# A filter-then-SiLU kernel: the first batch's rows stored in two halves, the second batch's x loaded ahead of the weights, weight rounding moved between steps

## The chip, the cores and the metric

The kernel runs on one core of a Trainium2 chip. The metric is the device time of one execution in microseconds (us); the median of three runs of the kernel before is 2508.29 us (2508.0 to 2508.46). One more execution was taken under the hardware profiler; the lines and times below are of that one, counted from the start of its span.

## What is computed

Two blocks follow one another. The first filters x along its 3008 positions in the frequency domain, the second is a feed-forward block with SiLU on every row of the result:

```python
X = np.fft.rfft(x, axis=1)                       # x: (8, 3008, 256)
y = np.fft.irfft(X * (filt_r + 1j * filt_i), n=3008, axis=1)
h = y.reshape(8 * 3008, 256) @ w_in              # w_in: (256, 2048)
out = (h / (1 + np.exp(-h))) @ w_out             # w_out: (2048, 256)
```

x and the filter are single precision, the weights arrive as double precision and are rounded to single precision on the chip.

## The kernel before, in words

**Main loop.** After a start of some 60 us, TensorE runs 384 steps (`hidden` and `project`, L966 and L1025): 8 batches, two halves each, three blocks of token pairs per half, eight steps of weights per block. A step multiplies by `w_in` with seven products in place of eight (sums of blocks are formed on VectorE), applies SiLU on ScalarE, and multiplies by `w_out`, one step behind. VectorE adds the sums that TensorE's next product waits for (L950). Every engine executes its own instructions in program order, so whatever is written between two of them is in the way of the later one.

**Filter of the next batch.** It is cut into pieces that are written into the steps by hand: `put(step, round, piece)` places a piece at one of eight rounds of a step. The filter is a transform in two stages with a filter product between: stage 1 (matmuls into tiles `pa`), rows stored to DRAM (`d1`) and loaded turned, `forward` (`pb`), `multiply`, `inverse` (`pc`), rows stored to DRAM (`d2`) and loaded turned (tiles `t4`), and `stage3` (`pd`), whose result y feeds the main loop.

**First batch.** Nothing runs beside it, so its chain is on the way to step 0. Its six groups g go through `inverse_first` and `rows_first` (L664): two tiles of 128 partitions per group are copied out of PSUM and stored to `d2`, 256 KB each. The first 32 positions split into two halves, n below 16 and n from 16. `load_t4_rows(k)` (L699, L703) loads the first half only, three loads of two DMAs, from SP (k = 0 and 2) and POOL (k = 1). `stage3(0..3)` then makes the first half of y. The second half of `d2` is loaded by `load_t4(g)` from step 8 on (L694).

**Order of DMA issues around it.** SP issues the tables, weights 0 to 3, then the second batch's x for two stage-1 pieces (`load_two`, L405), then weights 4 and 5 (L1302 to L1315). Stores of `rows_first` go out on ScalarE's queue, and for two tiles on SP's. While `d2` is stored and loaded TensorE runs a filler, `idle(11, small=20)` (L1362): products whose result nobody reads.

**After pd.** POOL copies one element of y to `gate` (L1365), so that its later DMAs stay behind y. Then it issues `store_rows(0)` and `store_rows(1)` (L426, L429): the stage-1 rows of the second batch, four DMAs of 96 KB each per piece. The tiles t1 that they read come from a pool of two. Piece u = 2 of stage 1 (TensorE L416, ScalarE copies L421) stands in step 1, one more piece in each step up to step 6. Its copy into t1 needs the first t1 tile back, that is, the landing of the four DMAs of `store_rows(0)`. SP meanwhile issues x for u = 2, weights 6 and 7, x for u = 3, weights 8, 9 and 10.

**Rounding of weights.** Weights 4 to 15 are rounded during steps 0 to 9, in pieces on VectorE: `bits` (two instructions), `added`, `signed`, `placed` (one each; `rounded` is `added` and `signed`), with `converted` on ScalarE, and `combine_weights` (four additions) for each pair. The table that places them is at L1382 to L1397.

**Semaphores of DMAs.** There are eight of them for the hardware queues (SP and ScalarE together) and eight for POOL's, used in turn. A DMA waits until the one that had its semaphore before has landed.

Of the kernel before, what the change touches and what calls it, by code (L numbers as in the profile page):

```python
# [46 lines left out]
FP32 = mybir.dt.float32  # L47
# [6 lines left out]
B, S, C = 8, 3008, 256  # L54
DFF = 2048
N1, N2 = 47, 64
NS, NG = 24, 6
# [106 lines left out]
def dft_tables():  # L164
# [22 lines left out]
    n = np.arange(32)[:, None]  # L187
    for par in range(2):
        for i, idx in enumerate(ORDER):
# [3 lines left out]
            k = np.where((kap - sp) % 94 == 0, kap, S - kap)  # L193
# [5 lines left out]
    e = np.zeros((4, 32, NG, 2, 2, 2, 32))  # L199
    n = np.arange(32)[None, :]  # L200
    for g in range(NG):
        for bank in range(2):
            for j in range(4):
# [3 lines left out]
                k = np.where((kap - s) % N1 == 0, kap, S - kap)[:, None]  # L207
# [57 lines left out]
def kernel(  # L265
# [9 lines left out]
    nc = tc.nc  # L275
# [84 lines left out]
    def spectral(b):  # L360

        if b > 0:
            d1 = dpool.tile([2, NS, 2, 32, C], FP32, name=f"d1_{b}", tag="d1")
        d2 = dpool.tile([2 * NS, 32, 2, C], FP32, name=f"d2_{b}", tag="d2")
        xs, us, t2s, banks, prods, halves, t4s = {}, {}, {}, {}, {}, {}, {}
# [298 lines left out]
        def rows_first(g):  # L664

            if g in (2, 3):
                room = t4pool.tile([128, 4, C], FP32, name=f"q_{b}_{g}", tag="t4")
                tiles = room[:, 0:2], room[:, 2:4]
            else:
                tiles = [pool.tile([128, 2, C], FP32, name=f"q_{b}_{g}_{i}", tag=tag) for i, (pool, tag) in  # L670
                         enumerate(((zpool, "z"),) * 2 if g == NG - 1 else ((qpool, "q"), (opool, "o")))]
            for i, qt in enumerate(tiles):
                copy, queue = (nc.scalar.copy, nc.scalar) if i == 0 or g < 4 else (nc.scalar.copy if g == 4 else nc.vector.tensor_copy, nc.sync)
                copy(out=qt, in_=halves[g][i])
                a0 = 8 * g + 4 * i
                queue.dma_start(out=d2[a0:a0 + 4].rearrange("a n h c -> (a n) h c"), in_=qt)

# [16 lines left out]
        def load_t4(g):  # L694
            t4s[g] = t4pool.tile([128, 4, C], FP32, name=f"t4_{b}_{g}", tag="t4")
            for h in range(2):
                nc.sync.dma_start(out=t4s[g][64 * h:64 * h + 2 * NS], in_=d2[:, 4 * g:4 * g + 4, h, :])

        def load_t4_rows(k, queue=None):  # L699

            first, by = SPREAD[k]
            for h in range(2):
                (queue or nc.sync).dma_start(out=us["t4"][64 * h + first:64 * h + first + 15 * by + 1:by],  # L703
                                  in_=d2[16 * k:16 * k + 16, 0:16, h, :])

# [34 lines left out]
        def load_wide(k):  # L740
            t4s[k] = [t4pool.tile([128, 8, C // 2], FP32, name=f"t4_{b}_{k}_{cb}", tag="t4") for cb in range(2)]
            for cb in range(2):
                for r in range(4):
                    nc.sync.dma_start(
                        out=t4s[k][cb][32 * r:32 * r + 24],
                        in_=d2[r % 2::2, 8 * k:8 * k + 8, r // 2, 128 * cb:128 * cb + 128])

# [31 lines left out]
        def fold_wide(k, h):  # L779
# [3 lines left out]
            for at, n, op in ((0, 24, ALU.add), (24, 23, ALU.subtract)):  # L783
                nc.vector.tensor_tensor(out=dst[:, :, :, at:at + n], in0=even[:, :, :, 0:n], in1=odd[:, :, :, 0:n], op=op)

        return dict(us=us, store_rows=store_rows, evict_y=evict_y, halves=halves, load_first=load_first, stage1_first=stage1_first, load_x=load_x, load_two=load_two, stage1=stage1, reverse_x=reverse_x,
                    load_fold=load_fold, fold=fold, stage1_fold=stage1_fold, evict_fold=evict_fold, pairs_fold=pairs_fold, forward_two=forward_two, free_two=free_two, multiply_two=multiply_two, add_two=add_two, inverse_two=inverse_two, even_two=even_two, rows_two=rows_two, ends_two=ends_two,
# [436 lines left out]
    def weights(*js, queue=None):  # L1224
        for j in js:
            if wide:
                load_weights(j, queue)
# [73 lines left out]
    nc.sync.dma_start(out=wi_t, in_=ws_dram.ap())  # L1301
    weights(0, 1, 2, 3)  # L1302

# [8 lines left out]
    for j in range(4):  # L1312
        part["stage1_first"](j)
    second["load_two"]()
    weights(4, 5)  # L1315
    part["forward"](0, fill=12)
# [44 lines left out]
    placed(2, 3)  # L1361
    idle(11, small=20)  # L1362
    for g in range(4):
        part["stage3"](g)
    gp.tensor_copy(out=gate, in_=y[0, 0][:, 0, 28:29])  # L1365
    for u in range(2):
        second["store_rows"](u)
    idle_wide(1)
    nc.sync.dma_start(out=wi_t, in_=wi_dram.ap())
    second["load_x"](2)  # L1370
    weights(6, 7)
    second["load_x"](3)
    early[0] = None
    plan_rest(0, part)
# [7 lines left out]
    for step, rnd, *todo in (  # L1382
            (0, 1, (combine_weights, 1), (bits, 4)), (0, 5, (converted, 4), (bits, 5), (added, 4)),
            (1, 0, (converted, 5), (weights, 8, 9, 10)), (1, 1, (signed, 4), (placed, 4), (rounded, 5), (placed, 5)),
            (1, 5, (combine_weights, 2)),
            (2, 1, (bits, 6), (added, 6)), (2, 5, (converted, 6), (bits, 7)), (3, 0, (converted, 7)),
            (3, 1, (signed, 6), (placed, 6), (added, 7)), (3, 5, (signed, 7), (placed, 7)), (3, 7, (bits, 8)),
            (4, 0, (converted, 8), (weights, 11)), (4, 1, (rounded, 8), (placed, 8), (bits, 9)), (4, 2, (weights, 12)),
            (4, 5, (converted, 9), (added, 9), (bits, 10)), (5, 0, (converted, 10), (weights, 13)),
            (5, 1, (signed, 9), (placed, 9), (rounded, 10), (placed, 10)),  # L1390
            (5, 5, (combine_weights, 3)), (5, 7, (bits, 11)), (6, 0, (converted, 11), (weights, 14, 15)),
            (6, 1, (rounded, 11), (placed, 11), (bits, 12)), (6, 5, (converted, 12), (combine_weights, 4)),
            (6, 7, (bits, 13)), (7, 0, (converted, 13)),
            (7, 1, (rounded, 12), (placed, 12), (rounded, 13)), (7, 5, (combine_weights, 5)), (7, 7, (bits, 14)),
            (8, 0, (converted, 14)), (8, 1, (placed, 13), (rounded, 14), (placed, 14), (bits, 15)),
            (8, 5, (converted, 15), (combine_weights, 6)),
            (9, 1, (rounded, 15), (placed, 15)), (9, 5, (combine_weights, 7))):  # L1397
        for piece, *args in todo:
            put(step, rnd, piece, *args)
# [7 lines left out]
    for pair in range(len(pairs)):  # L1407
        step, rnd = combines[pair % per] if pair not in (1, 2) else ((2, 1), (11, 5))[pair - 1]
        pending.append((pair // per * STEPS + step + rnd / ROUNDS, 98, lambda pair=pair: tokens(pair)))
        for chunk in range(2 if pair < len(pairs) - 1 else 0):  # L1410
            step, rnd = stores[pair % per][chunk] if pair > 1 else (stores[1 - pair][chunk] if pair == 0 else (13, 1 + 4 * chunk))
            pending.append((pair // per * STEPS + step + rnd / ROUNDS, 99 + chunk,
                            lambda pair=pair, chunk=chunk: output(pair, chunk)))
# [65 lines left out]
```

## Time and profile before

| | us |
|---|---|
| median of three runs | 2508.29 |
| the profiled execution | 2507.81 |
| its span | 2506.0 |
| TensorE busy in the span | 2485.5 |
| VectorE busy | 1758.7 |
| ScalarE busy | 1097.1 |
| POOL busy | 433.3 |
| last pd product of the start ends | 59.41 |
| first product of step 0 starts | 60.15 |

The profile gives for each engine its busy time and, for each instruction, when it ran, on which line, from which tiles to which, and what ended the idle time before it. A single-precision product appears as two matmul records, so "x22" is 11 products. Queue q1 holds SP's DMAs, q10 ScalarE's and q0 POOL's. "SPq", "ACTq" are the sequencers that issue DMAs. The trace also holds each DMA packet with its queue, start and size, and each landing of a DMA as an update of its semaphore.

### The profile page before, as it was taken

The page shows a single profiled execution, that of the slowest core. Times are in us where ns is not written, and L with a number is a line of the kernel's source. Part 1 is how long each engine was busy: PE and PEld are TensorE (multiplying, and loading weights), DVE is VectorE, ACT ScalarE, POOL GpSimd, SP SyncE. Part 2 cuts the span into 40 slices and gives each one's busy share as a digit, 9 for nine tenths or more (in the row PEclk, how much of TensorE's full clock was granted, in tenths as well). Part 3 has the DMA queues.
Part 4 walks back from the last instruction along what each step waited for, and adds up shares of the span by engine and source line. Part 5 has one row for each costly group of instructions (what it writes and reads, how often), then busy time and mean ns, then how long its engine had stood idle before and what let it go on. Part 6 is the DMA issues. An engine that isn't in the chain of part 4 may idle for free.

```text
span 2506.0 us, 42288 instructions
## 1 busy us (share of the span) xinstructions
PE 2485.5 (99%) x16240; PEld 2126.6 (85%) x16240; DVE 1758.7 (70%) x3608; ACT 1097.1 (44%) x3006; POOL 433.3 (17%) x675
## 2 busy tenths in 40 slices
PE   8999999999999999999999999999999999999999
PEld 6678888888888888888888888888888888888988
DVE  6876677777767777777777867777677767655544
ACT  3644444444444444444444444444444444444443
POOL 3211212112121121211222112211121111101100
PEclk9999999999999999999999999999999999999999
DMA  7523232213232032420324203321142211200000
GB/s 277 181 69 98 71 83 63 77 51 80 60 88 77 26 90 51 116 65 16 88 66 106 57 26 85 84 68 43 31 108 56 55 43 34 64 21 9 17 9 17
DMA packets 139705, 170.67 MB, mean 68 GB/s; under 512 B 20892, under 2 KB 112892, under 8 KB 138876
## 3 DMA queue, kind: packets, MB, share of 16 engines
q1 hardware_dynamic: 115536, 120.49, 18.3%
q0 software_dynamic: 22240, 44.63, 6.9%
q8 instruction: 127, 2.08, 0.4%
q10 hardware_dynamic: 1728, 2.87, 0.3%
q14 instruction: 74, 0.61, 0.1%
HBM read 96.06 MB, written 81.26 MB: 71 GB/s over the span
## 4 chain that ended last, share of the span: by engine, by line
PE 97%; DVE 2%; ACT 0%; DMA 0%; issue 0%; POOL 0%; SPq 0%; DVEq 0%; ACTq 0%
PE acc L1047 45%; PE px L979 26%; PE pyz L979 19%; PE pd L754 1%; PE pf L486 1%; PE pc L582 1%; PE pb L544 1%; DVE g L950 0%; PE pa L392 0%; PE pc L660 0%; PE pa L416 0%; PE pd L718 0%; PE pb L526 0%; DMA w_t<-d 0%; PE pc L640 0%
## 5 line engine op out<-in xcount | busy, mean ns | idle before, releaser
L1047 PE MATMUL acc<-g,w_t 128*128 128x256 f32 (+1 forms) x5376 | 1507.7, 376 | 3.0 <-ACT o L767 2.5
L1047 PEld LDWEIGHTS acc<-g,w_t 128*128 128x128 f32 x5376 | 1016.0, 190 | 154.4 <-ACT o L767 15.3
L950 DVE TENSOR_TENSOR g<-pyz,abc 128x256 f32<-128x256 f32 (+1 forms) x1152 | 479.2, 416 | 475.1 <-ACT abc L1000 237.0
L950 DVE TENSOR_TENSOR g<-g 128x256 f32<-128x256 f32 (+3 forms) x1152 | 589.8, 512 | 196.8 <-ACT g L983 183.7
L979 PE MATMUL px<-ty,w_t 128*128 128x256 f32 (+1 forms) x2304 | 676.0, 375 | 0.6 <-ACT abc L1000 0.5
L983 ACT ACTIVATE g<-g 128x256 f32<-128x256 f32 (+1 forms) x1152 | 472.9, 411 | 239.3 <-DVE g L950 239.3
L950 POOL TENSOR_TENSOR s<-s 128x256 f32<-128x256 f32 (+1 forms) x322 | 247.1, 785 | 1386.1 <-DVE s L1073 991.4
L979 PEld LDWEIGHTS px<-ty,w_t 128*128 128x128 f32 x2304 | 434.0, 190 | 58.1 <-issue 3.7
L979 PE MATMUL pyz<-y,w_t 128*128 128x256 f32 (+1 forms) x1536 | 451.7, 376 | 3.7 <-DVE g L950 3.6
L979 PEld LDWEIGHTS pyz<-y,w_t 128*128 128x128 f32 x1536 | 283.0, 189 | 48.6 <-DVE g L950 8.5
L994 ACT COPY abc<-px 128x256 f32<-128x256 f32 (+1 forms) x384 | 141.5, 369 | 367.7 <-PE px L979 367.7
L983 ACT ACTIVATE g<-px 128x256 f32<-128x256 f32 (+1 forms) x384 | 146.0, 380 | 298.7 <-PE px L979 298.6
L1000 ACT COPY abc<-px 128x256 f32<-128x256 f32 (+1 forms) x384 | 141.7, 369 | 307.8 <-PE px L979 307.7
L979 PE MATMUL px<-y,w_t 128*128 128x256 f32 (+1 forms) x768 | 227.4, 378 | 0.9 <-ACT g L983 0.8
L979 PE MATMUL pyz<-ty,w_t 128*128 128x256 f32 (+1 forms) x768 | 226.0, 376 | 0.6 <-DVE g L950 0.6
L979 PEld LDWEIGHTS px<-y,w_t 128*128 128x128 f32 x768 | 143.4, 189 | 24.5 <-ACT g L983 3.3
L979 PEld LDWEIGHTS pyz<-ty,w_t 128*128 128x128 f32 x768 | 141.9, 190 | 23.0 <-DVE g L950 3.0
L987 ACT COPY abc<-px 128x256 f32<-128x256 f32 (+1 forms) x384 | 135.5, 353 | 36.2 <-PE px L979 36.2
L506 POOL DMA_DIRECT2D d<-tf x96 | 48.6, 506 | 212.7 <-DVE tf L436 212.7
L1073 ACT COPY s<-acc 128x512 f32<-128x512 f32 (+1 forms) x92 | 53.1, 577 | 46.5 <-issue 28.1
L603 POOL DMA_DIRECT2D d<-low x36 | 22.3, 618 | 291.8 <-DVE low L599 286.1
L476 DVE TENSOR_TENSOR uf<-x_all 120x512 f32<-120x512 f32 (+1 forms) x72 | 60.2, 863 | 0.3 <-issue 0.3
(130 smaller groups left out, 1359.7 us busy)
## 6 DMA issues: line engine op xcount, KB each, us to landing
t<-d SPq DMA_DIRECT2D x84, 256.0 KB
t<-d SPq DMA_DIRECT2D x224, 96.0 KB
out_dram<-s SPq DMA_DIRECT2D x62, 256.0 KB
d<-q POOLq DMA_DIRECT2D x48, 256.0 KB, 5.2
x_all<-in_x_dram SPq DMA_DIRECT2D x96, 96.0 KB
x_all<-xr SPq DMA_DIRECT2D x96, 96.0 KB
d<-tf POOLq DMA_DIRECT2D x96, 96.0 KB, 2.7
d<-tq POOLq DMA_DIRECT2D x96, 96.0 KB, 2.9
```

The costliest lines, as they stand in the source:

```text
L476: nc.vector.tensor_tensor(out=out, in0=in0, in1=in1, op=op)
L486: nc.tensor.matmul(out=ps[q][32 * k:32 * k + 32], lhsT=wq_t[rows, k], rhs=rhs[k][rows], start=True, stop=True)
L506: nc.gpsimd.dma_start(out=d1[par, :, grp, at:at + 4], in_=part[rows].rearrange("p q n c -> p (q n) c"))
L544: nc.tensor.matmul(out=ps[k, ri][32 * j:32 * j + 32, a, :], lhsT=dn_t[rows, 4 * (g + a) + at, :], rhs=t2s[g + a][rows, at, :], start=True, ...
L950: eng.tensor_tensor(out=out, in0=in0, in1=in1, op=op)
L979: nc.tensor.matmul(out=out, lhsT=w_t[:, jp, c, 0], rhs=rhs, start=start, stop=True, skip_group_check=True)
L983: nc.scalar.activation(out=g[:, k, 0:n], in_=g[:, k, 0:n] if src is None else src, func=AFT.Silu)
L987: nc.scalar.copy(out=sums[:, 0, 0:n], in_=xo)
L994: nc.scalar.copy(out=sums[:, 1, 0:n], in_=xo)
L1000: nc.scalar.copy(out=sums[:, 2, 0:n], in_=xo)
L1047: nc.tensor.matmul(out=acc[pair][i][:, h, 0:n], lhsT=w_t[:, jp, OUT_PLACE.get(c, c), 1], rhs=g[:, k, 0:n], start=(new and h == 0), stop=la ...
L1073: copy(out=dst, in_=src)
```

## The change

`rows_first` keeps its tiles and stores only the even partitions (the first half of the positions, since the table e is permuted so that the two halves alternate). A new `store_half(g, i, 1, gp)` stores the odd partitions from POOL, for all twelve tiles, after `gate` and ahead of `store_rows`. `d2` of the first batch has the half as its leading index. For the second batch, which shares the table e, `load_wide` picks every other row. The tiles of groups 4 and 5 sit in other pools or in free space of `w_t`.

`load_two` moves ahead of weights 0 to 3, weights 4 and 5 follow those directly. Of SP's loads after pd, x for u = 3 now comes ahead of weights 7. Weights 7 and 8 use tiles of the pool t4 that the tiles of groups 2 and 3 occupy until both halves are stored. The filler becomes 24 small and 6 larger products in place of 20 and 11. The table of rounding pieces is rewritten.

```diff
-    n = np.arange(32)[None, :]
+    n = np.arange(32).reshape(2, 16).T.reshape(1, 32)
...
-        d2 = dpool.tile([2 * NS, 32, 2, C], ...)
+        d2 = dpool.tile([2 * NS, 32, 2, C] if b else [2, 2 * NS, 16, 2, C], ...)
...
         def rows_first(g):
...
+            us["q", g] = tiles
             for i, qt in enumerate(tiles):
...
                 copy(out=qt, in_=halves[g][i])
-                a0 = 8 * g + 4 * i
-                queue.dma_start(out=d2[a0:a0 + 4].rearrange("a n h c -> (a n) h c"), in_=qt)
+                store_half(g, i, 0, queue)
+
+        def store_half(g, i, half, queue):
+
+            a0 = 8 * g + 4 * i
+            queue.dma_start(out=d2[half, a0:a0 + 4].rearrange("a n h c -> (a n) h c"), in_=us["q", g][i][half::2])
...
+            first = 16 * (k % 2) + k // 2
+            rows = slice(8 * k, 8 * k + 8) if b > 1 else slice(first, first + 15, 2)
...
     nc.sync.dma_start(out=wi_t, in_=ws_dram.ap())
-    weights(0, 1, 2, 3)
+    second["load_two"]()
+    weights(0, 1, 2, 3, 4, 5)
...
-    second["load_two"]()
-    weights(4, 5)
     part["forward"](0, fill=12)
...
-    idle(11, small=20)
+    idle(6, small=24)
     for g in range(4):
         part["stage3"](g)
     gp.tensor_copy(out=gate, in_=y[0, 0][:, 0, 28:29])
+    for g in (2, 3, 4, 5, 0, 1):
+        for i in range(2):
+            part["store_half"](g, i, 1, gp)
     for u in range(2):
         second["store_rows"](u)
...
     second["load_x"](2)
-    weights(6, 7)
+    weights(6)
     second["load_x"](3)
+    weights(7)
...
-            (1, 5, (combine_weights, 2)),
-            (2, 1, (bits, 6), (added, 6)), (2, 5, (converted, 6), (bits, 7)), (3, 0, (converted, 7)),
...
+            (1, 3, (bits, 6), (added, 6)), (1, 5, (converted, 6), (combine_weights, 2)),
+            (2, 1, (signed, 6), (placed, 6), (bits, 7), (added, 7)), (2, 5, (converted, 7), (bits, 8), (weights, 11)),
...
-            (7, 1, (rounded, 12), (placed, 12), (rounded, 13)), (7, 5, (combine_weights, 5)), (7, 7, (bits, 14)),
-            (8, 0, (converted, 14)), (8, 1, (placed, 13), (rounded, 14), (placed, 14), (bits, 15)),
-            (8, 5, (converted, 15), (combine_weights, 6)),
-            (9, 1, (rounded, 15), (placed, 15)), (9, 5, (combine_weights, 7))):
+            (7, 0, (converted, 14)), (7, 1, (signed, 13), (placed, 13), (rounded, 14), (placed, 14)),
+            (7, 5, (combine_weights, 5)), (7, 7, (bits, 15)), (8, 0, (converted, 15)),
+            (8, 1, (rounded, 15), (placed, 15)), (8, 5, (combine_weights, 6)), (9, 5, (combine_weights, 7))):
```

TensorE's order of instructions is the same in both kernels but for the number of fillers. ScalarE's copy of stage-1 piece u = 2 waits for the same four DMAs as before; in POOL's order twelve DMAs of 128 KB now stand ahead of them.

## The prediction

> **What bounds the kernel now.** I read the page first, then TensorE's timeline of the start, then the issues and DMA packets around it, then who waits for whom in steps 0 to 9.
>
> ```profile
> PE 2485.5 (99%) x16240; PEld 2126.6 (85%) x16240; DVE 1758.7 (70%) x3608; ACT 1097.1 (44%) x3006; POOL 433.3 (17%) x675
> ...
> PE 97%; DVE 2%; ACT 0%; DMA 0%; issue 0%; POOL 0%; SPq 0%; DVEq 0%; ACTq 0%
> ```
>
> TensorE is the chain. Its products don't change, so only its idle time of 20.5 us (2506.0 - 2485.5) and slow stretches can move; the change can win or lose a handful of us. Its start:
>
> ```profile
> 45.14 1.45 PE L1276 MATMUL idle<-wx_t 32*32 32x32 f32 x40
> 46.52 2.72 PE L1278 MATMUL idle<-wx_t 96*128 96x128 f32 x22
> 51.36 0.29 PE L718 MATMUL pd<-wi_t,w_t 64*64 64x47 f32 x2 [2.12 <-ACT t L421]
> 52.31 5.53 PE L718 MATMUL pd<-wi_t,w_t 64*64 64x47 f32 x252 [0.66 <-DMA w_t<-d]
> 59.15 0.26 PE L718 MATMUL pd<-wi_t,w_t 64*64 64x47 f32 x2 [1.32 <-issue]
> ```
>
> The filler ends at 49.24 and pd stands until 52.31. The first wait is named after ScalarE, but both end as a load of t4 lands (51.12 and 52.07 by the DMA semaphores), so it is the DMA. The issues behind it (SP, ScalarE, SP):
>
> ```profile
> 42.04 0.84 SPq L676 DMA_DIRECT2D d<-q  x2
> ```
> ```profile
> 43.84 0.33 ACTq L676 DMA_DIRECT2D d<-q  x1
> ```
> ```profile
> 47.16 1.20 SPq L703 DMA_DIRECT2D w_t<-d  x2
> ```
>
> The last load goes out at 47.16, as the last store lands (47.14). That store was issued at 43.84 although its tile was ready at 42.5: its semaphore was that of load 0, which landed at 43.77, having been issued at 39.59 when the fourth store landed (39.52).
>
> After pd, POOL's queue and ScalarE's copies of piece u = 2:
>
> ```profile
> 60.30 4.14 POOL L429 DMA_DIRECT2D d<-t  x8
> ```
> ```profile
> 70.30 0.59 ACT L421 COPY t<-pa 128x512 f32<-128x512 f32 x1 [1.47 <-PE pa L416]
> 71.16 0.59 ACT L421 COPY t<-pa 128x512 f32<-128x512 f32 x1 [0.27 <-PE pa L416]
> 71.64 0.38 ACT L1000 COPY abc<-px 128x256 f32<-128x256 f32 x1
> ```
>
> The copy at 70.30 needs the first four of the eight stores landed. The semaphores have them at 65.54, 68.66, 69.08 and 69.81: 0.5 us to spare. Why so late, shows in the packets of 66 to 70, and of 47 to 48, where POOL's queue is alone:
>
> ```profile
> DMA packets 570, 1.61 MB, mean 404 GB/s; under 512 B 179, under 2 KB 179, under 8 KB 569
> ...
> q1 hardware_dynamic: 303, 1.08, 67.7%
> q0 software_dynamic: 266, 0.52, 34.0%
> ```
> ```profile
> DMA packets 90, 0.29 MB, mean 295 GB/s; under 512 B 18, under 2 KB 18, under 8 KB 90
> ```
>
> The DMA engines are full, and POOL's q0 gets 0.13 MB/us beside SP's 0.27.
>
> Last, waits of TensorE for VectorE in 69 to 120 and 120 to 131:
>
> ```profile
> PE pyz L979 <- DVE g L950: 0.9, 3, 0.5
> ```
> ```profile
> PE pyz L979 <- DVE g L950: 2.0, 4, 0.8
> ```
>
> **The change, part by part.** *Stores at the start.* Twelve stores shrink from 256 to 128 KB. The first four then are 0.52 MB instead of 1.05; at 0.39 MB/us (1.55 MB in 34 to 38) that is 1.35 us, and fewer bytes stand ahead of load 0, which I put 2 us earlier (issue 37.5, landing 41.6). Then nothing holds the last store: issue at 42.5, 1.3 us earlier. It took 3.3 us to land in traffic; with half the bytes I estimate 2.3, so 44.8 and the last load 2.4 us earlier. The load itself (4.0 and 4.3 us) has less beside it: 0.2. pd starts at 49.7, a gain of **2.6**. Bounds: 1.3 if only the last four stores' bytes count; 4.0 if TensorE's inverse of group 5 also comes sooner (a 0.97 us issue gap at 37.2 stands in full DMA traffic). With the DMA gone, next late is ScalarE's row: its t1 copies ended at 51.74, before pd's fourth bank; they also move up by 1.3, being queued behind the store's issue.
>
> *Filler.* Four small products more (0.07 each), five larger fewer (0.25 each): it ends at 48.3, still ahead of pd. Nothing by itself.
>
> *Clock.* The trace grants half clock from 52.08 for 3.41 us, 2.84 us after the filler's end. pd's 252 records took 5.53 us; 62 of the same kind at 153.47 took 1.17, so 252 would take 4.76. With 1.4 us of idleness instead of 2.8 I count this **0.8** as won (bounds 0 and 0.8).
>
> *x ahead of the weights.* TensorE reaches stage 1 at 41.5, x landed at 34.69: nothing won. Weights 0 land some 2 us later (0.79 MB at 0.4 MB/us) than 25.57, and are read from 38.4. Nothing lost. The other rows that batch 1's `load_wide` picks are as many and as long, and issued twelve steps ahead of need: nothing, and if it shows, tenths.
>
> *Later halves behind pd.* Twelve POOL DMAs of 128 KB, 1.57 MB, now stand in q0 ahead of the 0.39 MB of `store_rows(0)`. POOL's issue takes 0.54 us for a like store (L692), 6.5 us in all, but the queue is slower. By the clock of before (pd's end at 59.41): q0's first packets came at 64. SP has three loads, 1.31 MB, 0.81 of them moved by 64, the rest by 65.9; in that time q0 moves 0.13 MB as before. Then weights 7 waits for the first two later halves, and q0 is alone until its packets start at 67.9, 2 us at 0.29 to 0.4 MB/us: 0.85 MB in all. The remaining 1.11 MB run beside weights 7 to 10 and x, 2.49 MB. At 0.13 MB/us that ends at 76.4, landing 77; if the larger DMAs (128 KB against 96) raise the share by a third, at 75.2. I take a landing at 76.3. The copy wants it at 70.30: a wait of **6.0** us on ScalarE. Queued behind it are the copy at 71.64 and the SiLUs; TensorE's next px product ran at 72.26, 0.24 us after that copy, so nearly all of the wait is TensorE's. Bounds: nothing if q0 could move all 1.97 MB by 69.8 (0.34 MB/us, its rate alone); 9.7 us at 0.13 MB/us from 64 on.
>
> The Trainium skill (DMA: Bandwidth & Descriptors, Queues, rings and completion order) says that each DMA engine takes turns between queue rows, a packet at a time. Were turns equal in bytes, q0 would get half, which is the second rival below; the trace has it at a third.
>
> SP's own new wait, for weights 7, holds weights 8 to 10 and x for u = 4 behind it. Weights 7 are read at 78 (`bits`, step 2), that x at 85: covered, since the issue comes back at 66.6.
>
> *Clock after that wait.* 6 us of idleness is twice what lowered the clock at the start; 3.4 us at half cost 1.7 of dense products. Part may fall into the wait: **1.5** (bounds 0 and 2.5). The Trainium skill (TensorE: Matmul & The Clock Gate, What's actually happening) gives about 3.4 us for a window of its monitor; the trace's 3.41 agrees.
>
> *Roundings.* By issue distances `bits` takes 0.67 us, `added`, `signed` and `placed` 0.6 each, a combine 1.5. A step's own VectorE work is 2.4 and a forced wait of 0.5 (for SiLU). Steps 1 to 6, with pa, are 7.8 us long and leave 4.9; later ones are 6.06 and leave 3.1. Weights' work before, in steps 7, 8, 9: 5.1, 4.5, 3.3, too much by 3.5 in sum, for waits of 2.0 and 0.4 (ScalarE's g behind it). After: 5.1, 3.3, 1.5, too much by 2.1: 1.2 us won. Step 1 goes from 4.5 to 5.7, over by 0.8, but that lies beside ScalarE's wait; steps 2 to 6 have 4.6, 4.3 and a drain, 3.7, 5.1, 4.6. Of the 0.9 us in 69 to 120 I count 0.3 as won. Sum **1.5** won (bounds 0.8 lost, if the wait's cover in step 1 is gone and its delay reaches the last product of the step; 3.3 won).
>
> Sum: -2.6 - 0.8 + 6.0 + 1.5 - 1.5 = +2.6. The execution was 2507.8 (span 2506.0 and 1.8 around it), 0.5 below the median: 2510.4, or 2510.9 as a median. A measurement can tell about 0.2% (5.0 us) from no change: 2503.3 to 2513.3 counts as the same.
>
> **Rivals.** *No wait at step 1:* SP, held back by the later halves, leaves q0 alone, and the t1 rows land in time. For it: alone q0 moves 0.29 MB/us and more. Against: 66 to 70. The gains stand: -4.9, 2503.4; with the full bounds 2500; I say 2502.5.
>
> *Equal turns:* q0 gets 0.2 MB/us from 67.9, landing at 74.1, a wait of 3.8 and 1.0 of clock: -0.1, 2508.2. For it: in the microsecond from 81 both queues move 0.12 MB; against: the third in 66 to 70, four times as long.
>
> *Slower, q0 starved:* POOL's twelve DMAs wait for each other's semaphores eight apart, q0 runs dry while SP's five loads are queued, and the wait is 9 to 9.7 with 2.5 of clock; with 2.6 and 0.8 won at the start and 1.5 at the roundings, +7 or so, 2515.5. It decides from a wait of 7.9 on: there the gains of 4.9 and 5.0 us are used up with 2.0 of clock. For it: the first rows took 5.2 to 8.6 us to land with nothing ahead of them.
>
> *The start does not shorten:* load 0 is held by something else than bytes, and the last store keeps its time: +6.0, 2514.
>
> **Chances.** Forecast 0.40, no wait 0.15, equal turns 0.20, starved 0.20, no shorter start 0.05. The first lies within 0.2% but for 0.04, no wait is beyond it in 0.12, equal turns in 0.01, starved in 0.17: faster 0.13, same 0.61, slower 0.26. The range takes in most of the first rival and of the starved one: 2503 to 2517.
>
> **What would show it.** pd starting at 49 to 50.5 at full clock; POOL's twelve d<-q from about 57.5 and the first d<-t some 8 us behind gate; ScalarE's copy of u = 2 waiting on a DMA of d<-t for 4 to 8 us and TensorE idle with it, a half clock behind; shorter waits for VectorE in the steps after the last pa. I am wrong if that copy starts within 12 us of pd's end, or pd's start hasn't moved.

## The result and the profile after

The changed kernel takes 2514.86 us (median of 12 runs, 2512.5 to 2516.66), the kernel before 2508.43 (12 runs beside them, 2507.38 to 2511.57): a ratio of 1.0025, 95% interval 1.0016 to 1.0034. It is slower by 6.4 us, just beyond the 5 us that the prediction counted as no change. The profiled execution took 2514.95 us, its span 2513.0. The page of the changed kernel has the same TensorE time as before; what was added is idle time and slow clock:

```profile
PE 2484.8 (99%) x16238; PEld 2127.2 (85%) x16238; DVE 1760.7 (70%) x3608; ACT 1095.1 (44%) x3006; POOL 438.4 (17%) x687
...
PE 96%; DVE 2%; DMA 1%; ACT 0%; issue 0%; POOL 0%; SPq 0%; DVEq 0%; ACTq 0%
```

**Where along the execution.** Both kernels run the same 1536 SiLU activations on ScalarE, four per step, in one order. Subtracting the start times of the same activation in the two traces tells how far the changed kernel lags at that point: -0.52 us at the first (step 0), +9.10 at the ninth (step 2), +6.86 at the 41st (step 10), +6.93 at the last. So the start won 0.5, steps 0 and 1 lost 9.6, steps 2 to 9 won 2.2, and the other 374 steps did nothing. These columns return for each experiment below.

**The start.** TensorE's timeline of the changed kernel (start, length, line, tiles, and in brackets the idle time before and what ended it):

```profile
43.91 1.70 PE L1286 MATMUL idle<-wx_t 32*32 32x32 f32 x48
45.54 1.60 PE L1288 MATMUL idle<-wx_t 96*128 96x128 f32 x12
51.48 0.42 PE L726 MATMUL pd<-wi_t,w_t 64*64 64x47 f32 x2 [4.34 <-DMA w_t<-d]
52.22 5.98 PE L726 MATMUL pd<-wi_t,w_t 64*64 64x47 f32 x254 [0.32 <-DMA w_t<-d]
...
59.80 0.60 PE L989 MATMUL px<-y,w_t 128*128 128x256 f32 x2
```

The filler ends at 47.14, earlier than before (49.24), but pd stands until 52.22, where it was 52.31. Load 1 (POOL) and the last load, load 2 (SP), were issued at:

```profile
44.73 1.37 POOL L711 DMA_DIRECT2D w_t<-d  x2 [8.37 <-DMA d<-q]
```
```profile
45.41 1.22 SPq L711 DMA_DIRECT2D w_t<-d  x2
```

The last load went out 1.75 us earlier than before, and landed at 51.98 instead of 52.07: its two DMAs took 5.8 and 6.0 us instead of 4.0 and 4.3. Load 1 went out 1.0 later (43.72 before).

**Ahead of the start.** One difference between the executions belongs to no edit. TensorE's stage 1 of the first batch (`pa`, L392, the same 96 records in every kernel), in the kernel before, in the changed kernel and in e9 below:

```profile
6.50 11.43 PE L392 MATMUL pa<-w_t,wx 32*128 32x512 f32 x96
```
```profile
6.26 10.83 PE L392 MATMUL pa<-w_t,wx 32*128 32x512 f32 x96 [0.33 <-DMA w_t<-in_x_first_dram]
```
```profile
6.50 12.66 PE L392 MATMUL pa<-w_t,wx 32*128 32x512 f32 x96
```

Until the trace first grants full clock one of these records takes some 1.06 us, from then on 0.59. That moment is 7.70 us into the span before, 5.11 in the changed kernel and 10.19 in e9; in the fourteen traces it lies anywhere from 5.1 to 10.2. So `pb`, the next stage, starts at 17.86, 17.01 and 19.09, before anything that the change touches on TensorE, and a lag at step 0 of a microsecond or two in a single trace can't be credited to an edit. The table of the experiments gives the start of `pb` beside the lag.

**Step 1.** POOL's timeline behind pd:

```profile
58.90 0.18 POOL L1374 COPY gate<-y 128x1 f32<-128x1 f32 x1 [12.80 <-DVE y L740]
59.13 3.22 POOL L684 DMA_DIRECT2D d<-q  x6
62.35 1.24 POOL L684 DMA_DIRECT2D d<-w_t  x2
65.08 0.54 POOL L684 DMA_DIRECT2D d<-q  x1 [1.49 <-DMA d<-q]
67.16 1.59 POOL L684 DMA_DIRECT2D d<-q  x3 [1.54 <-DMA d<-q]
68.75 2.52 POOL L429 DMA_DIRECT2D d<-t  x5
```

The ninth of the later halves waits for the semaphore of the first, the tenth for that of the second. The rows, `d<-t`, which the eight issues of before had out by 64.4, go out from 68.75 on, and the first four have landed at 77.46 (69.81 before). Who waits for them, on ScalarE and then on TensorE:

```profile
77.60 1.07 ACT L421 COPY t<-pa 128x512 f32<-128x512 f32 x2 [9.40 <-DMA d<-t]
```
```profile
79.00 1.22 PE L989 MATMUL px<-ty,w_t 128*128 128x256 f32 x2 [7.22 <-ACT abc L1010]
```

The copy follows the landing by 0.14 us; before, it stood at 70.30 and waited for TensorE alone. The windows of the changed kernel (stretch, length, then busy us and count for PE, PEld, DVE, ACT and POOL, the granted clock, the DMA share and GB/s) show what came behind:

```profile
70.00:79.00 9.00, 1.78 (x8) 1.03 (x6) 2.54 (x6) 1.40 (x4) 2.80 (x7) 0.88 0.93 363
79.00:84.00 5.00, 5.00 (x13) 4.05 (x14) 2.95 (x7) 2.68 (x6) 1.93 (x4) 0.54 0.33 83
84.00:100.00 16.00, 15.49 (x63) 11.35 (x61) 14.71 (x31) 9.85 (x22) 4.01 (x8) 1.00 0.44 137
```

In the first the DMA engines are full (0.93) and TensorE idles; in the second TensorE is busy throughout, on little more than half the products that it would otherwise do. The half clock lasts from 76.79 to 83.62; a pair of records takes 1.06 us where it takes 0.59, and pairs start 0.85 us apart where they start 0.43 apart.

### The profile page after: what moved, and what is told of

It is laid out like the page before. It is cut to its first block, busy times and chain, and to the rows that moved or that the text cites. A ratio compares the mean times of both kernels' runs of the same rounds, so it can differ in the third digit from the quotient of the medians.

```text
span 2513.0 us, 42305 instructions
## 1 busy us (share of the span) xinstructions
PE 2484.8 (99%) x16238; PEld 2127.2 (85%) x16238; DVE 1760.7 (70%) x3608; ACT 1095.1 (44%) x3006; POOL 438.4 (17%) x687
## 4 chain that ended last, share of the span: by engine, by line
PE 96%; DVE 2%; DMA 1%; ACT 0%; issue 0%; POOL 0%; SPq 0%; DVEq 0%; ACTq 0%
PE acc L1057 45%; PE px L989 25%; PE pyz L989 19%; PE pd L764 1%; PE pf L486 1%; PE pc L582 1%; PE pb L544 1%; DVE g L960 1%; PE pc L660 0%; PE pa L392 0%; PE pd L726 0%; PE pb L526 0%; DMA d<-t 0%; DMA d<-q 0%; DMA w_t<-d 0%
```

## The experiments

Each is timed beside the kernel before, in 10 or 11 runs; "pb" is where `pb` starts (before 17.86, the changed kernel 17.01), and "lag" the lag against the profiled execution of before at step 0, step 2, step 10 and the last SiLU, as above (the changed kernel: -0.5, +9.1, +6.9, +6.9).

| run | median us | ratio, interval | pb | lag |
|---|---|---|---|---|
| e1 rows first | 2505.35 | 0.9986 (0.9977 to 0.9994) | 17.23 | -2.0, -1.1, -3.1, -3.2 |
| e2 table only | 2507.42 | 0.9995 (0.9986 to 1.0004) | 18.96 | +0.4, +1.4, -0.7, -0.6 |
| e3 x behind | 2515.06 | 1.0022 (1.0013 to 1.0031) | 17.03 | -1.8, +9.2, +7.0, +7.0 |
| e4 six ahead | 2506.75 | 0.9992 (0.9983 to 1.0001) | 17.08 | -1.3, +2.8, +0.6, +0.6 |
| e6 loads back | 2506.61 | 0.9986 (0.9977 to 0.9995) | 17.24 | -1.7, -0.4, -2.5, -2.3 |
| e7 filler | 2505.16 | 0.9984 (0.9976 to 0.9993) | 16.83 | -2.9, -1.8, -3.9, -3.8 |
| e8 four on SP | 2508.70 | 0.9997 (0.9988 to 1.0006) | 16.91 | -0.7, +4.0, +1.8, +1.5 |
| e9 halves only | 2507.55 | 0.9992 (0.9983 to 1.0001) | 19.09 | -0.4, -0.3, -0.3, -0.6 |
| e10 weights on POOL | 2511.05 | 1.0007 (0.9998 to 1.0016) | 17.28 | -0.0, +7.1, +4.9, +5.0 |
| e11 before, filler | 2508.09 | 0.9997 (0.9988 to 1.0006) | 17.01 | -0.9, -0.9, -0.9, -0.8 |
| e12 filler, late rows | 2515.07 | 1.0025 (1.0015 to 1.0034) | 17.89 | -1.8, +8.5, +6.3, +6.3 |
| e13 load alone | 2509.70 | 1.0001 (0.9992 to 1.0010) | 19.00 | +2.8, +4.3, +2.2, +1.9 |

By the intervals e1, e6 and e7 are faster than the kernel before, e3 and e12 slower; the others can't be told from it.

### The wait: the place in POOL's queue (e1, e4)

e1 is the changed kernel with the rows issued ahead of the later halves:

```diff
+    for u in range(2):
+        second["store_rows"](u)
     for g in (2, 3, 4, 5, 0, 1):
...
-    for u in range(2):
-        second["store_rows"](u)
```

> The changed kernel with store_rows(0) and (1) issued by POOL ahead of the twelve later halves; all else as changed. If the place in POOL's queue is the cause: ScalarE's copy of piece u = 2 starts without a DMA wait, some 9 us behind the end of pd, no half clock falls into step 1, and the 9 us lost there are back: 2505 to 2507. If it is the 1.57 MB more in that stretch, in whatever order: the copy still waits 3 us or more, 2510 to 2514.

The copy of u = 2 in e1, on ScalarE's timeline, waits for TensorE alone again, and no half clock follows:

```profile
68.17 0.59 ACT L421 COPY t<-pa 128x512 f32<-128x512 f32 x1 [1.47 <-PE pa L416]
```

The 1.57 MB of later halves are still stored in the same steps, so it was not their bytes, but their place ahead of the rows. Putting the rows first turned the change from 0.25% slower into 0.14% faster than before, inside the range of the first theory.

e4 puts six of the twelve halves ahead of the rows and six behind:

```diff
-    for g in (2, 3, 4, 5, 0, 1):
-        for i in range(2):
-            part["store_half"](g, i, 1, gp)
+    later = [(g, i) for g in (2, 3, 4, 5, 0, 1) for i in range(2)]
+    for g, i in later[:6]:
+        part["store_half"](g, i, 1, gp)
     for u in range(2):
         second["store_rows"](u)
+    for g, i in later[6:]:
+        part["store_half"](g, i, 1, gp)
```

> The changed kernel with six of the twelve later halves (0.79 MB) ahead of store_rows and six behind. Queue order, with q0 at 0.13 MB/us beside SP and 0.3 to 0.4 alone: the wait of piece u = 2 is 1 to 3 us in place of 7, too short for a long stretch of half clock: 2507 to 2510. Bytes of the stretch in any order: the wait stays 5 to 7 us, 2513 to 2515.

TensorE's wait in e4:

```profile
73.26 0.70 PE L989 MATMUL px<-ty,w_t 128*128 128x256 f32 x2 [2.11 <-ACT abc L1010]
```

The wait is that of queue order (1 to 3 us), and a half clock of 3.41 us followed it; the time of 2506.75 lies just below that theory's range. From POOL's first issue behind pd to the landing of the four rows: 9.1 us with none ahead (57.22 to 66.30), 12.8 with six (58.96 to 71.76), 18.3 with twelve (59.13 to 77.46): 0.6 to 0.9 us for each half of 128 KB ahead.

### Who slows POOL's queue (e8, e10)

e8 takes four halves out of POOL's queue and puts them on SP's, behind its load of wi_t:

```diff
-    for g in (2, 3, 4, 5, 0, 1):
+    for g in (4, 5, 0, 1):
...
+    for g in (2, 3):
+        for i in range(2):
+            part["store_half"](g, i, 1, nc.sync)
```

> The changed kernel with the later halves of groups 2 and 3 on SP's queue, behind its load of wi_t, and eight left on POOL's queue ahead of store_rows. The bytes stay the same, and SP's own 0.52 MB come ahead of weights 7 to 10. Theory (POOL's queue has 1.57 MB ahead of the rows, at 0.13 MB/us beside SP's, and its ninth to twelfth DMA wait on semaphores of the first, when it ran dry for 2 us): 0.52 MB less and no dry stretch, so the t1 rows land 2 to 4.5 us earlier, at 73 to 75.5; ScalarE's copy of u = 2 waits 3 to 5 us rather than 9.4, TensorE 2 to 4; 2509.5 to 2512.5 us. Rival (the place in the queue does not matter, the engines are full and the bytes set the landing): still at 77, 2514.9.

```profile
75.85 0.70 PE L989 MATMUL px<-ty,w_t 128*128 128x256 f32 x2 [3.45 <-ACT abc L1010]
```

The rows landed at 74.34, inside the theory's range, and TensorE's wait (3.45) too; ScalarE's copy waited longer than expected (6.42), and the time came out lower, 2508.7; no half clock followed this wait, where 6.83 us of it followed that of the changed kernel. The same bytes in another queue cost 3.8 us less wait: again the place, not the bytes.

e10 leaves the halves and gives weights 7 to 10 to POOL behind the rows, so that SP has nothing to load beside them:

```diff
-    weights(7)
+    weights(7, queue=gp)
...
-            (1, 0, (converted, 5), (weights, 8, 9, 10)), ...
+            (1, 0, (converted, 5), (lambda *js: weights(*js, queue=gp), 8, 9, 10)), ...
```

> The changed kernel, with weights 7 to 10 issued from POOL's queue behind the rows instead of from SP's, so that SP's queue has nothing left to load from about 65 until x for u = 4. The twelve later halves stay ahead of the rows. Theory (the rows land late because q0 shares the engines with SP's weights 7 to 10, at 0.13 MB/us): q0 alone moves its remaining 1.8 MB at 0.3 to 0.4 MB/us, the rows land at 71 to 73 by the clock of the changed kernel, ScalarE's copy of u = 2 waits 3 to 5 us rather than 9.4, TensorE 1 to 3 rather than 7.2, no half clock follows; 2505 to 2509 us. Rival (POOL's DMAs wait for each other's semaphores, eight apart, and the dry 2 us of q0 come from that whatever SP does): the rows at 75 to 77, TensorE's wait 5 us or more, 2511 to 2515.

```profile
77.18 1.22 PE L989 MATMUL px<-ty,w_t 128*128 128x256 f32 x2 [4.90 <-ACT abc L1010]
```

Nearer the rival: the rows landed at 75.63 and the time of 2511.05 lies in its range, with a wait of 4.9 just below its 5. The rows landed 15.6 us after POOL's first issue (59.99 to 75.63) rather than 18.3, so by these two executions SP's weights account for some 2.7 us, and a half clock of 6.83 us followed. The rest goes with POOL's own pace: alone from 68 to 72, q0 moved 0.14 to 0.26 MB/us, and POOL issues one DMA each 0.5 us (128 KB in 0.54, 96 KB in 0.5: 0.24 and 0.20 MB/us). In 72 to 74 the x for u = 4 (0.39 MB) took q1 again. Neither theory alone holds: both the sharing and the pace of issues and semaphores are in it. How much of the rest is issues and how much semaphores, no run tells.

### The start (e3, e6, e9, e13)

e3 is the changed kernel with x for u = 0 and 1 behind weights 3, as before:

```diff
-    second["load_two"]()
-    weights(0, 1, 2, 3, 4, 5)
+    weights(0, 1, 2, 3)
...
     for j in range(4):
         part["stage1_first"](j)
+    second["load_two"]()
+    weights(4, 5)
```

> The changed kernel with x back behind weights 3. If x ahead holds ScalarE's second store (its semaphore was that of x, landing at 30.2), the stores of groups 0 and 1 and load 0 go out about 1 us earlier, and step 0 starts 0.5 to 1.5 us earlier: 2513.4 to 2514.5. If the start is set by the sum of the bytes alone: no difference, 2514.5 to 2515.3.

Its first product of step 0 came at 58.53, 1.3 us before that of the changed kernel; the rows landed at 77.49, as there, TensorE waited 8.35, and the lag from step 2 on is the same. What the start wins is taken back where step 1 waits for the rows, so the time of 2515.06 is the rival's. The theory's reason fails too: none of the four stores that load 0 waits for stood for a semaphore in e3, and load 0 still went out at 39.11 (39.05 in the changed kernel).

e9 is the halves alone: the edits of e1 and e3, and the table (with the place of the piece of output) and the order of weights 6 and 7 as before, with

```diff
-    idle(6, small=24)
+    idle(11, small=20)
```

> The halves alone: first halves stored and loaded as in the change, the later halves on POOL's queue behind the rows of the second batch's stage 1; x behind weights 3, the filler, the table of roundings and the order of weights 6, 7 as before. It tells how the gain of the rows first (3.4 us) splits. Theory: the halves are worth some 1.5 us at the first product of step 0 (58.5 against 60.15), the table and tokens some 1 to 1.3 us later on, so 2506.5 to 2507.3 us here. Rival (the table hides the cost of the later halves in steps 1 to 6, and without it they cost there): 2508 or more. Second rival (the halves are worth nothing at the start without x ahead of the weights): the first product of step 0 at 59.8 or later, 2508.

The first product came at 59.75: of the 2.0 that e1's execution had won at step 0, 0.4 are there, a hair short of the second rival's 59.8, and the time of 2507.55 lies between the theory's range and the rivals'. But in this execution `pb` started at 19.09, 1.9 us behind that of e1, by the clock alone, so the trace doesn't tell what the halves are worth at the start. The medians fit the theory better: 0.08% for the halves here and 0.05% for the table (e2) are together about the 0.14% of e1, though neither alone is clear of the noise. From step 0 to step 10 nothing changes, so the later halves cost nothing when they are behind the rows.

e6 is e1 with x behind weights 3 and weights 4 and 5 behind load 2:

```diff
-    second["load_two"]()
-    weights(0, 1, 2, 3, 4, 5)
+    weights(0, 1, 2, 3)
...
     for j in range(4):
         part["stage1_first"](j)
+    second["load_two"]()
...
     part["load_t4_rows"](2)
+    weights(4, 5)
```

> The kernel with the rows of the second batch's stage 1 ahead of the later halves, and with SP's loads of the start put out of the way of the stores: x for u = 0 and 1 behind weights 3 as before, weights 4 and 5 behind the last load of t4. Theory (ScalarE's stores wait for semaphores that SP's loads used last, so the start's gain was lost to x and weights 4 and 5 landing 0.5 to 1 us later): the last store is issued 1 to 2 us earlier, pd starts at 48 to 49.5 and the first product of step 0 at 56 to 57.3, against 58.30 with the rows first alone; 2504 us or less. Rival (the 1 KB packets of load 0 and load 1 or TensorE's own inverse set the time): pd at 50 and the first product of step 0 at 58.3 as with the rows first alone, 2505.3. Weights 4 are read in steps 0 and 1, so a wait of VectorE there would show that they came too late.

Half of the theory held: load 0 went out at 35.37 and load 1 at 42.02 (39.05 and 44.73 in the changed kernel), so SP's loads had been holding them. Whether by their semaphores or by their bytes e6 doesn't separate, since it takes both away: no store waited for a semaphore, and the four that load 0 waits for landed 2.9 to 5.5 us behind their issue rather than 5.2 to 6.5. For load 0 the bytes are the likelier, as e3 had no such semaphore either. But the last store went out at 41.69 (41.80 in e1), as TensorE finished its inverse no earlier, and load 2, beside weights 4, needed 6.4 us (43.95 to 50.34). First product at 58.63, near the rival's 58.3, in 2506.61 us.

e13 is e1 with x behind weights 3; it moves weights 4 and 5 to POOL's queue, ahead of load 1, and takes 12 fillers. Of its edit:

```diff
+    weights(4, 5, queue=gp)
     part["load_t4_rows"](0)
     part["load_t4_rows"](1, nc.gpsimd)
```

> The kernel with the rows first, x for u = 0 and 1 behind weights 3, and weights 4 and 5 issued from POOL's queue at about 36.5, ahead of load 1 of t4, so that they have landed when load 2 runs and SP's queue has nothing left that holds the stores; 12 larger filler products (the filler ends at about 48). Theory (the start's gain was lost to the last load, which in the changed kernel runs beside load 1 and took 6 us rather than 4.8, since load 1 goes out no earlier than before): load 1 goes out at 42 to 42.5, load 2 at 44 to 44.7 and takes 4.3 to 5 us, pd starts at 48.5 to 49.7 and the first product of step 0 at 55 to 56.5, against 58.30 with the rows first alone and 57.21 with the longer filler; 2503 to 2504.5 us. Rival (the two loads share what the engines move of 1 KB packets however they are placed, or weights 4 and 5 stand in the way of load 1 in POOL's queue): the last load lands at 50.5 or later, the first product at 57 or later, 2505 or more.

A miss: the weights ran in q0 at 0.17 to 0.31 MB/us from 41 to 45, beside the last stores, the store that load 2 waits for landed at 49.03, and both loads went out half a microsecond apart. POOL's, SP's and TensorE's timelines:

```profile
48.63 1.18 POOL L711 DMA_DIRECT2D w_t<-d  x2 [8.98 <-DMA d<-q]
```
```profile
49.12 1.22 SPq L711 DMA_DIRECT2D w_t<-d  x2
```
```profile
55.77 6.39 PE L726 MATMUL pd<-wi_t,w_t 64*64 64x47 f32 x254 [0.34 <-DMA w_t<-d]
```

Step 0 then starts late, and the last line tells what e13 was to tell, in the opposite direction: two loads side by side need 7 us from load 1's issue. What a last load takes that is early and alone, no run shows. Over all executions with this start (the changed kernel, e1, e4, e7, e8, e10, e12): load 1 goes out at 42.6 to 45.1 (mean 44.1), load 2 at 44.7 to 45.9 (mean 45.4), and the last load lands 7.0 to 8.0 us behind load 1's issue, 5.3 to 6.8 behind its own, at 51.5 in the mean. With the start of before (before, e2, e11): load 1 at 43.9, load 2 at 47.4, landed 4.4 to 5.0 us behind its own issue, at 52.2. Load 2 moved up by 2.0 us, load 1 not at all, and the time until both have landed moved by 0.8.

### The clock (e7, e11, e12)

e7 is e1 with 17 larger fillers instead of 6:

```diff
-    idle(6, small=24)
+    idle(17, small=24)
```

> The kernel with the rows first, and 17 larger filler products in place of 6 (11 more of 0.25 us, so that the filler ends at about 49.9 rather than 47.1 and pd, ready at 50.1, follows at once). Theory (the half clock around pd comes from the idle stretch ahead of it): no half clock between 47 and 57, pd's 252 records at 4.8 us rather than 5.5, the first product of step 0 at 57.3 to 57.8 rather than 58.30, 2504.3 to 2504.8 us. Rival (the half clock comes whatever stands there, or the filler's end pushes pd back): the first product of step 0 at 58.2 or later, 2505.3 or more.

```profile
45.22 4.06 PE L1288 MATMUL idle<-wx_t 96*128 96x128 f32 x34
50.13 0.29 PE L726 MATMUL pd<-wi_t,w_t 64*64 64x47 f32 x2 [0.84 <-ACT t L421]
50.81 3.70 PE L726 MATMUL pd<-wi_t,w_t 64*64 64x47 f32 x232 [0.40 <-DMA w_t<-d]
...
57.21 0.67 PE L989 MATMUL px<-y,w_t 128*128 128x256 f32 x2
```

e1's second group of pd:

```profile
50.81 5.49 PE L726 MATMUL pd<-wi_t,w_t 64*64 64x47 f32 x254 [0.30 <-DMA w_t<-d]
```

pd starts when e1's did (50.81 in both), no half clock is granted, its records take 16 ns each instead of 22 (3.70 / 232 against 5.49 / 254 in e1), and step 0 starts 1.1 us earlier. The theory held in this execution; e12, with the same filler, still had a half clock of 3.41 us from 52.13. In the time it shows less: 2505.16 against 2505.35, whose intervals overlap. e1 and e7 are both faster than either kernel; which of the two is faster, the runs don't tell.

e11 is the kernel before with 20 larger fillers instead of 11:

```diff
-    idle(11, small=20)
+    idle(20, small=20)
```

> The kernel before with 20 larger filler products in place of 11 (the filler ends at about 51.5 rather than 49.2, as the first load of t4 lands). Theory (the half clock at pd comes from the idle stretch ahead of it, in the kernel before too): no half clock between 48 and 60, pd's 252 records at 4.8 us rather than 5.5, the first product of step 0 0.5 to 1 us earlier than 60.15, 2507.4 to 2508.2 us, within what can be told. Rival (the filler's end pushes pd back, or the half clock comes anyway): the first product of step 0 at 60.2 or later, 2508.7 or more.

The first product came at 59.25, as the theory had it, but not for its reason: the filler ended at 50.98, the load landed late, and a half clock of 3.41 us still came at 53.68, with pd's records as slow as before (5.54 us for 254). What e11's trace lacks is the 1.32 us in front of the last two records of pd in before, an idle stretch that nothing in the profile ends. e11 says nothing on the clock; its time can't be told from that of before.

e12 is the changed kernel with e7's edit of the filler alone, the rows still behind the halves.

> The changed kernel with 17 larger filler products in place of 6, the rows still behind the later halves. With the rows first the same filler took 1.1 us off the first product of step 0. Theory (POOL's queue starts at pd's end but moves at the pace of SP's loads, so an earlier step 0 waits the longer for the rows): first product of step 0 at 57.2 to 58.7, TensorE's wait for ScalarE's copy of u = 2 at 7.2 to 8.7 us, the rows landed within 0.5 us of 77.5; 2514 to 2515. Rival (the rows move up with pd's end): the wait stays at 7.2 or below, rows at 76 to 76.5, 2513.5 or less.

Step 0 started at 58.33, 1.5 us before that of the changed kernel; the rows landed at 77.02 and TensorE waited 7.9 us. As expected, the gain ahead of the wait is lost in it: 2515.07 us.

Over all executions the half clock around pd lasted 6.83 or 10.24 us in the seven with 6 fillers, 3.41, 6.83 and 3.41 with the 11 of before (before, e2, e9), 6.83 with 12 (e13), and none, 3.41 and 3.41 with 17 or 20 (e7, e12, e11). A longer filler shortens it; it doesn't remove it for certain.

### The roundings (e2)

e2 is the kernel before with the new table and the new place of one piece of output, and nothing else:

```diff
-            (1, 5, (combine_weights, 2)),
-            (2, 1, (bits, 6), (added, 6)), (2, 5, (converted, 6), (bits, 7)), (3, 0, (converted, 7)),
...
+            (1, 3, (bits, 6), (added, 6)), (1, 5, (converted, 6), (combine_weights, 2)),
+            (2, 1, (signed, 6), (placed, 6), (bits, 7), (added, 7)), (2, 5, (converted, 7), (bits, 8), (weights, 11)),
...
-        step, rnd = combines[pair % per] if pair not in (1, 2) else ((2, 1), (11, 5))[pair - 1]
+        step, rnd = combines[pair % per] if pair not in (1, 2) else ((2, 3), (11, 5))[pair - 1]
```

> The kernel before with the new table of roundings alone (and the sums of the second token block at round 3 of step 2). If the moved roundings are a gain of their own: TensorE's waits for VectorE in steps 7 to 9 shrink from 2.4 to 0.7 us as in the changed kernel, and those of steps 1 to 6 stay below 1 us: 2506 to 2507.5. If the wait of piece u = 2 hid an overload of step 1: new waits of 0.5 to 1.5 us in step 1, 2507.5 to 2509.

Its lag grows by 1.1 us from step 0 to step 2, then falls by 2.1 to step 10. TensorE's waits for VectorE from 79 to 131, before and in e2:

```profile
PE pyz L979 <- DVE g L950: 2.9, 7, 0.8
```
```profile
PE pyz L979 <- DVE g L950: 1.7, 4, 0.7
```

The fuller step 1 costs 1.1 us, steps 2 to 9 bring 2.1, of which 1.2 in the emptier steps 7 to 9. Both theories came in part: the later waits shrank and step 1 got a new one, and 2507.42 lies near the border of the two ranges. In the changed kernel the first is hidden beside the wait for the rows, and all of the second is left (+9.10 to +6.86).

## Why the prediction was right and wrong

The forecast, 2510.9 with a range of 2503 to 2517, had the sign of its sum right and its size too small: +2.6 forecast, +6.4 measured in the medians, +6.9 and +7.0 in the two traces' lag and spans. The time lies in the range, but beyond the forecast's own bound for the same. Of the 4.3 us that the sum misses against the lag, 2.9 are the start with its clock, 2.1 the wait with its clock, and the roundings take 0.7 back. Term by term:

- **The wait** was right in place and mechanism: e1 removes it by order alone, e4 and e8 shrink it. It was 7.2 us on TensorE, not 6.0; ScalarE's copy, for which the 6.0 was worked out, came 7.9 us later behind its product than in before (77.60 with the product at 68.61, where it was 70.30 with 69.24). The landing was put at 76.3, some 16.9 us behind pd's end; it came 19.3 behind (58.20 to 77.46). The share of 0.13 MB/us beside SP held (0.12 to 0.16 in 72 to 77). What failed is the stretch "q0 is alone": it did move 1.0 MB in 65 to 68, but then ran dry (8 KB in 68, nothing in 69), as POOL's DMAs waited for their own semaphores and for 0.5 us each. That was the mechanism of the starved rival; q0 was dry for about 2 us only, so its wait of 9 or more did not come, but the 7.9 of the copy stand where the prediction let that rival begin.
- **The clock behind the wait** was right, some 2.3 us (the five pairs from 79.00 took 4.43 us, the same ones from 72.26 in before 2.16) where 1.5 was forecast. Together with the wait: 9.6 lost, 7.5 forecast.
- **The start** failed: -2.6 and -0.8 forecast, -0.5 in this execution. By the prediction's own sign it was wrong here: pd's start hasn't moved (52.22, before 52.31). The five executions with exactly this start and filler (the changed kernel, e1, e4, e8, e10) have a lag of -2.0 to -0.0 at step 0, -0.9 in the mean; the two of the old start 0 and +0.4; so some 1.1 us, with a scatter as large, and not even that is shown to be the change's, since full clock came earlier in the five (`pb` at 16.91 to 17.28) than in the two (17.86 and 18.96). The chain up to the last issue came near the forecast in their mean (last store 42.5, forecast 42.5; last load 45.5, forecast 44.8). The step that failed is "The load itself (4.0 and 4.3 us) has less beside it: 0.2": 5.8 and 6.0 us here. It had more beside it: load 1, which hadn't moved; that this is the cause fits all executions, but no run has the last load early without load 1 beside it. Load 1 waits for the second store of group 3, and that went out at 39.99, later than in before (39.26), behind a store that stood until 38.87 for the semaphore of weights 5; load 0's packets of 1 KB were ahead of it in the queues, as load 0 was only half a microsecond earlier (39.05, where the forecast's 37.5 rests on smaller stores). Four stores of this execution stood for semaphores that SP's x and weights 3 to 5 held (issued 30.28, 35.92, 37.03 and 38.87). For load 0 that isn't the whole of it, as e3 shows; with weights 4 and 5 out of the way (e6) it went at 35.37. "Next late" was load 1, and not ScalarE's row.
- **The clock at the start** had the wrong sign: the new filler ends 2.1 us earlier and pd no earlier, so TensorE idles 4.3 us, and the half clock lasts 6.83 us instead of 3.41 (pd 5.98 us, not 5.53). From that group to step 0 it was nonetheless 7.58 us, and 7.84 before, as the idle 1.32 us of before stand in it. "Nothing by itself" was wrong of the shorter filler: e7 points the same way from the other side, and so do the lengths over all executions, though e2 had 6.83 us with the filler of before as well.
- **The roundings** were right, with 2.2 won rather than 1.5, for the reason given: the fuller step 1 lies beside the wait. Where that cover is gone (e1, e2) the net gain is 1.1 and 1.0. Of the 2.2, the 1.2 of steps 7 to 9 are what was forecast for them; steps 2 to 6 brought 1.0 rather than 0.3.

"No wait at step 1" (2502.5) fell, as did "equal turns" (2508.2): in 70 to 77 of the changed kernel, by its DMA queues (packets, MB, share of the engines):

```profile
q1 hardware_dynamic: 512, 1.83, 68.0%
q0 software_dynamic: 398, 0.85, 30.9%
```

The Trainium skill (DMA: Bandwidth & Descriptors, Queues, rings and completion order) has the engines take turns between queues by packets. The trace agrees as far as both move all the time; the bytes are shared two to one, which the rule doesn't give. "The start does not shorten" (2514) came nearest term by term and had 0.05: its reason, that load 0 is held by something else than the stores' own bytes, is borne out by e6, and by e3 it is rather the traffic of SP's loads than their semaphores. The starved rival's 2515.5 was as near to the time, but by luck: it had some 2 us too much for the wait and its clock, and 2.9 too much won at the start.

TensorE reaches the second batch's stage 1 at 39.8 to 41.7, and two things in the traces add up to that: the start of `pb`, set by the clock as above, and an idle stretch of up to 1.53 us at about 37, which nothing in the profile ends (0.97 in before, 0.57 in the changed kernel, 1.53 in e3 and e11, none in e1, e2, e6, e9, e10, e12 and e13). The landing of the last load doesn't simply follow (52.70 in e11 with `pb` at 17.01, 51.93 in e2 with 18.96). Left open: what that stretch and the like one at pd are, and what scatters the last landing between 50.57 and 52.50 in executions of one start.

## What to carry to other kernels

Before DMAs are added to a queue, list what already stands behind the place and when it is wanted: here the same twelve stores cost 9.6 us ahead of eight small ones that the next step needed, and nothing behind them. When one of several loads that are waited for together is moved up, look where the others stand, since it then runs beside the one that didn't move: here the last load went out 2.0 us earlier and landed 0.8 earlier. And a gain ahead of a wait for a DMA is not a gain until the landing moves too.

## What the runs showed of the hardware

The half clock comes in spells of 3.41, 6.83 or 10.24 us, and two spells of one execution start whole multiples of 3.41 apart (49.48 and 76.79 in the changed kernel: 27.31, eight of them; 47.39 and 74.69 in e10). Whether an idle stretch draws one is not told by its length: e4's wait of 2.1 us (71.15 to 73.26) drew one at 74.31, e8's of 3.45 us drew none. Cut the traces into steps of 3.41 that end where a spell begins. In e8, counted on from its spell at 50.04, a step ends at 73.93, inside its wait, and so neither step has more than 1.9 us of it; e4's step of 70.90 to 74.31 holds all 2.1. Likewise a step with 1.96 us idle drew none in e12 (69.20 to 72.61). At the start, among the filler's products, less is enough: 0.62 us idle in e1's step of 43.90 to 47.31. The Trainium skill (TensorE: Matmul & The Clock Gate, What's actually happening) has a free-running window of 3413 ns, with which the spacing agrees; that an idle share below a whole window is enough, these runs show and the section doesn't say.

A store of half the size is not issued sooner: on ScalarE's queue its issue took 0.46 us, most of the larger ones of before 0.33.

Full clock is not there from the first product on, and it comes at another time in each execution: TensorE's first products, the same in all kernels here, start at 1.1 us, the first grant of full clock lies at 5.1 to 10.2, worth up to 1.8 us at the end of stage 1 (10.83 us in the changed kernel, 12.66 in e9).
